# Gates summed as logarithms, with TensorE adding up the first eight chunks

## The chip, the cores and the metric

The kernel runs on one core of a Trainium2 chip. The metric is the device time in microseconds (us). A core has TensorE (PE; its weight loads are listed as PEld), VectorE (DVE), ScalarE (ACT), GpSimd (POOL) and SyncE (SP, which issues the transfers here). Each works through its own queue in order and waits for the others by semaphores.

## The reference

A gated linear recurrence per head, and then a feed-forward block with the mish function on its outputs:

```python
f = 1.0 / (1.0 + np.exp(-f_logit))             # q, k, v, f_logit: (4, 8, 768, 48)
for t in range(S):
    state = f[:, :, t, :, None] * state + np.einsum('bhd,bhe->bhde', k[:, :, t], v[:, :, t])
    y[:, :, t] = np.einsum('bhd,bhde->bhe', q[:, :, t], state)
x = y.transpose(0, 2, 1, 3).reshape(B * S, H * D)   # 3072 tokens x 384
h = x @ w_in                                        # 384 -> 2048
g = h * np.tanh(np.log1p(np.exp(h)))                # h over 20 taken as it is
out = g @ w_out                                     # 2048 -> 384
```

## The kernel before

**Chunks.** The recurrence is cut into 24 chunks of 128 tokens: six blocks of tokens for each of four batches, chunk n being block n // 4 of batch n % 4. Within a chunk the product of the gates from the chunk's start, called the decay, turns the recurrence into matmuls: k is divided by the decay, q multiplied by it, and scores, a causal mask, and the state at the chunk's start give y. A chunk's tensors lie as 128 channels (two heads of 64 places) by 4 pairs of heads by 128 tokens, so 128 x 512.

For a chunk, `attend()` adds four steps to the plan. The first loads l (the logits, from fl), k and q (L333) and v (L336), and prepares them in `prep`. There ScalarE takes exp(-l) and adds one (L351, L352), VectorE makes the running product of these with a scan (L354), which is the inverse of the decay, and ScalarE takes its logarithm and the exponential of the negative (L357, L358), the decay, into a PSUM bank. A polishing step on VectorE follows: l becomes inverse times decay (L273), and L362 corrects the decay with that and flips its sign. k times the inverse runs on GpSimd (L273; on VectorE in chunk 0), q times the decay on VectorE (L273). L365 keeps the decay at the chunk's end. Chunks 0 to 3 are loaded and prepared in two halves of 256 columns, the rest in one piece.

The other steps: transposes of k (L410) and their copy (L413); the chunk's own update of the state (L427), the scores (L385) and the mask (L391), and mid and tmp, states within and after the chunk (L441, L444, L446); the outputs (L462, L474), the new state (L490), and the output's split into a high and a low part (L500, then L503 and L505 for chunks 0 to 3, L507 for the others), which together are the tile xt. Every four chunks make one group of 512 tokens; transfers (L513) fill the last places of xt, and only then can the feed-forward part take that group.

**The feed-forward part** runs over 96 units: a group g of 512 tokens by a slice j of 128 of the 2048 hidden columns. A unit is nine matmuls 128 x 512 into h (L212), nine steps of mish (L222 to L230) on ScalarE, VectorE and GpSimd, ending in g (L228) and its high and low parts (L229, L230), and nine matmuls into o (L235). Groups 0 and 1 take turns with half of the slices each, since the weights arrive and are split into high and low parts meanwhile (`split_w`: L316 and L323 on ScalarE; L318, L319, L321, L324 on VectorE); later groups have the weights at hand.

**Order.** All work is added to a `Plan` with estimated costs and the tiles it reads and writes; `Plan.order` packs it by a simulated list schedule and gives each engine's queue its order. `attend_goal(u)` says how many attention steps are added ahead of unit u. While TensorE has nothing to do at the start, `Plan.issue` puts filler matmuls on zeros into its queue (L304, fp32 128 x 128, two instructions each) up to the first unit's L235.

PSUM has three banks `at`, two `h` and three `o`. Chunks 0 to 3 use pairs of all three kinds, later chunks only the first two `at` banks, for the decay, then scores, then outputs; the third is for transposes and updates.

## Time and profile before

| | us |
|---|---|
| median of 3 runs | 536.96 (534.45 to 538.31) |
| the profiled execution | 537.24 |
| its span, first to last instruction | 535.5 |
| busy: TensorE, VectorE, ScalarE, GpSimd | 512.4, 382.8, 415.5, 174.2 |

The profile is one execution with a record for each instruction. Busy time is the time in which an engine had an instruction running; TensorE's matmuls overlap, and its fillers count as busy too. The granted TensorE clock is given as a share of 2.4 GHz; its mean was 0.994.

### The profile page before, as it was taken

To read this page: it belongs to the slowest core of one execution; us is meant where nothing else is said; L and a number is where in the kernel's file an instruction comes from. 1 tells how busy PE (TensorE), PEld (TensorE's weight loads), DVE (VectorE), ACT (ScalarE), POOL (GpSimd) and SP (SyncE) were. 2 spreads that over 40 slices of the span, in tenths; PEclk is the share of its full clock that TensorE was granted. 3 is DMA by queue.
4 is the path that set the end of the run, shared out by engine and by line. 5 is a ranking of instruction groups with operands and counts; after the bars stand their busy time and mean duration, and the time that the engine had idled before them with its cause. 6 is when DMAs were issued, how large, how long until landed. Compare 5 with 4: busy or idle time off the path is not lost.

```text
span 535.5 us, 13156 instructions
## 1 busy us (share of the span) xinstructions
PE 512.4 (96%) x5362; PEld 408.3 (76%) x5362; DVE 382.8 (71%) x617; ACT 415.5 (78%) x746; POOL 174.2 (33%) x153
## 2 busy tenths in 40 slices
PE   7899989899998999999999999999999999999992
PEld 7787767677777777787877777787787778788881
DVE  5988999999996878785767577747565763645441
ACT  7767877799878878878887878878788776777770
POOL 2311332233234434333443333333241322132330
PEclk9999999999999999999999999999999999999997
DMA  7876444424520443231213232202221000100001
GB/s 232 283 242 234 147 138 144 151 87 156 169 74 2 140 139 110 65 115 41 61 40 109 59 102 80 60 21 89 66 94 41 2 1 31 38 21 2 1 1 66
DMA packets 23926, 48.92 MB, mean 91 GB/s; under 512 B 2800, under 2 KB 6256, under 8 KB 23856
## 3 DMA queue, kind: packets, MB, share of 16 engines
q1 hardware_dynamic: 23856, 47.98, 28.1%
q8 instruction: 44, 0.72, 0.5%
q14 instruction: 26, 0.21, 0.1%
HBM read 39.32 MB, written 6.29 MB: 85 GB/s over the span
## 4 chain that ended last, share of the span: by engine, by line
PE 68%; DVE 16%; ACT 6%; DMA 4%; issue 4%; SPq 0%; DVEq 0%; ACTq 0%
PE h L212 31%; PE o L235 29%; DVE n L224 3%; DMA l<-fl 2%; DVE g L225 2%; DVE g L228 2%; PE at L427 2%; DVE wl L324 2%; PE at L462 2%; PE at L474 2%; DVE wt L319 2%; PE at L385 1%; DVE wt L321 1%; DMA xt<-xt 1%; PE at L410 1%
## 5 line engine op out<-in xcount | busy, mean ns | idle before, releaser
L230 POOL TENSOR_TENSOR gl<-g,gh 128x512 fp32r<-128x512 f32 x96 | 128.3, 1337 | 265.9 <-ACT gh L229 247.6
L212 PE MATMUL h<-xt,wh 128*128 128x512 f32 x576 | 185.2, 402 | 8.4 <-DVE g L228 5.3
L212 PEld LDWEIGHTS h<-xt,wh 128*128 128x128 f32 x576 | 104.6, 188 | 37.0 <-DVE g L228 9.2
L235 PE MATMUL o<-gh,wh 128*128 128x512 f32 x288 | 116.0, 403 | 0.0
L212 PE MATMUL h<-xt,wl 128*128 128x512 f32 x288 | 114.1, 396 | 0.1
L235 PE MATMUL o<-gl,wh 128*128 128x512 f32 x288 | 114.1, 396 | 0.0
L235 PE MATMUL o<-gh,wl 128*128 128x512 f32 x288 | 113.3, 393 | 0.0
L224 DVE SCALAR_TENSOR_TENSOR n<-n 128x512 f32<-128x512 f32 x96 | 70.7, 737 | 57.6 <-ACT n L223 57.5
L228 DVE TENSOR_TENSOR g<-g,h 128x512 f32<-128x512 f32 x96 | 65.2, 681 | 40.1 <-ACT h L227 39.7
L222 ACT ACTIVATE n<-h,hcap 128x512 f32<-128x512 f32 x96 | 65.7, 685 | 34.1 <-PE h L212 33.5
L226 ACT ACTIVATE h<-n,two 128x512 f32<-128x512 f32 x96 | 66.0, 688 | 22.7 <-DVE g L225 22.6
L229 ACT ACTIVATE gh<-g 128x512 fp32r<-128x512 f32 x96 | 60.3, 628 | 24.4 <-DVE g L228 22.2
L225 DVE TENSOR_TENSOR g<-h,n 128x512 f32<-128x512 f32 x96 | 66.0, 687 | 7.3 <-POOL gl L230 1.1
L223 ACT ACTIVATE n<-n,hcap 128x512 f32<-128x512 f32 x96 | 69.1, 720 | 2.0
L235 PEld LDWEIGHTS o<-gl,wh 128*128 128x128 f32 x288 | 54.1, 188 | 13.7 <-POOL gl L230 0.6
L212 PEld LDWEIGHTS h<-xt,wl 128*128 128x128 f32 x288 | 54.1, 188 | 13.7 <-DVE wl L324 0.5
L235 PEld LDWEIGHTS o<-gh,wh 128*128 128x128 f32 x288 | 54.1, 188 | 12.8 <-ACT ob L578 0.3
L235 PEld LDWEIGHTS o<-gh,wl 128*128 128x128 f32 x288 | 54.1, 188 | 12.4
L227 ACT ACTIVATE h<-h 128x512 f32<-128x512 f32 x96 | 55.9, 582 | 1.6
L273 POOL TENSOR_TENSOR k<-k,inv 128x512 f32<-128x512 f32 (+1 forms) x26 | 31.7, 1222 | 68.6 <-DVE inv L354 45.4
L354 DVE TENSOR_TENSOR_SCAN inv<-gate,ones 128x516 f32<-128x516 f32 (+1 forms) x28 | 31.7, 1132 | 3.4 <-ACT gate L352 3.4
L304 PE MATMUL o<-state 128*128 128x128 f32 x200 | 28.3, 297 | 1.1 <-DVE gate L288 1.1
(97 smaller groups left out, 517.1 us busy)
## 6 DMA issues: line engine op xcount, KB each, us to landing
raw<-ww SPq DMA_DIRECT2D x16, 768.0 KB, 4.7
v<-vn SPq DMA_DIRECT2D x24, 256.0 KB, 3.9
l<-fl SPq DMA_DIRECT2D x20, 256.0 KB, 2.7
k<-kk SPq DMA_DIRECT2D x20, 256.0 KB, 2.9
q<-qq SPq DMA_DIRECT2D x20, 256.0 KB, 3.3
out<-ob SPq DMA_DIRECT2D x18, 256.0 KB, 2.1
xt<-xt SPq DMA_DIRECT2D x15, 128.0 KB, 2.5
half<-ob SPq DMA_DIRECT2D x6, 256.0 KB, 2.3
```

The lines of the kernel that those rows point to most:

```text
L212: nc.tensor.matmul(h, w[:, j, a * P : (a + 1) * P], xt[:, x, a, :], start=(n == 0), stop=(n == 3 * NK - 1))
L222: ("act", T_ACT(GT, True, 1), 0, lambda: nc.scalar.activation(u, h, AF.Relu, bias=hcap, scale=-1.0)),
L223: ("act", T_ACT(GT, False, 1), 0, lambda: nc.scalar.activation(u, u, AF.Exp, bias=hcap, scale=-1.0)),
L224: ("dve", T_DVE(GT), 1, lambda: nc.vector.scalar_tensor_tensor(n, u, 2.0, u, ALU.add, ALU.mult)),
L225: ("dve", T_DVE(GT), 0, lambda: nc.vector.tensor_tensor(g, h, n, ALU.mult)),
L226: ("act", T_ACT(GT, False, 1), 0, lambda: nc.scalar.activation(h, n, AF.Ln, bias=two)),
L227: ("act", T_ACT(GT, True), 0, lambda: nc.scalar.activation(h, h, AF.Exp, scale=-1.0)),
L228: ("dve", T_DVE(GT), 0, lambda: nc.vector.tensor_tensor(g, g, h, ALU.mult)),
L229: ("act", T_ACT(GT), 0, lambda: nc.scalar.activation(gh, g, AF.Copy)),
L230: ("pool", T_POOL(GT), 1, lambda: nc.gpsimd.tensor_tensor(gl, g, gh.bitcast(F32), ALU.subtract)),
L235: nc.tensor.matmul(o, w[:, j, m * P : (m + 1) * P], x, start=(first and i == 0), stop=(last and i == 2))
L273: add("pool" if on_pool else "dve", cost, lambda: eng.tensor_tensor(dst, x, y, ALU.mult), reads, writes, port=port)
```

## The change

- Decays are summed as logarithms. The logit is held above -40 by VectorE (`F_MIN`), ScalarE takes exp(-l) and then ln(1 + .), and the running sum of that over tokens is the negative logarithm of the decay. Two exponentials give the inverse and the decay. The scan on products, the polishing product and its correction are gone, and the sign of the decay is no longer flipped (so mid, tmp and the final check of the chunk ends change signs).
- In chunks 0 to 7 (`NS`) the logits come with tokens on the partitions, from a new array ft made on the host. TensorE makes the running sum: for each pair of heads one fp32 matmul of the logarithms (as weights) with an upper triangle of ones, into the PSUM bank of the decay. This also brings the result to channels on the partitions.
- In chunks 8 to 23 VectorE makes the running sum by a scan (multiply by `go`, which is zero at each pair's first token, and add). The inverse lies in the second PSUM bank, and k times the inverse moves from GpSimd to VectorE.
- Only chunk 0 is loaded and prepared in two halves, before it was chunks 0 to 3.
- The order of the units (`TURNS`) is the same as before, written as a table. `attend_goal` adds the attention steps of chunks 4 to 7 and of chunks 12 to 23 one unit earlier.

```diff
-        (gate,), (inv1,) = (ring(nm, 1, [P, NP, C + 1]) for nm in ("gate", "inv"))
-        (kt_s,) = ring("kt", 1, [P, NP, C])
+        (kt_s,), (go,), (cum_,), (inv_s,) = (ring(nm, 1, [P, NP, C]) for nm in ("kt", "go", "cum", "inv"))
...
-            make_upper_triangular(nc, n_[0][:, 0:P], val=-1.0, diag=True)
+            make_upper_triangular(nc, tri, val=1.0, diag=True)
...
-        nc.vector.memset(gate[:, :, 0:1], 0.0)
+        nc.vector.memset(go, 1.0)
+        nc.vector.memset(go[:, :, 0:1], 0.0)
...
-                for nm, dst, src in (("l", l_, fl), ("k", k_, kk), ("q", q_, qq)):
+                for nm, dst, src in (("l", l_, ft if n < NS else fl), ("k", k_, kk), ("q", q_, qq)):
...
-                dec, kd = b[s0 // st].rearrange("p (a c) -> p a c", a=NP), [keys[s0 // st]]
-                add("act", T_ACT(w), lambda s=s: nc.scalar.activation(gate[:, s, 1:], f[:, s], AF.Exp, scale=-1.0), kf, kg)
-                add("act", T_ACT(w), lambda s=s: nc.scalar.activation(
-                    gate[:, s, 1:], gate[:, s, 1:], AF.Copy, bias=1.0), (), kg)
-                add("dve", 2 * T_DVE(w + st) - 70, lambda s=s, st=st: nc.vector.tensor_tensor_scan(
-                    inv1[:, s].rearrange("p a c -> p (a c)"), gate[:, s].rearrange("p a c -> p (a c)"),
-                    ones.broadcast_to([P, st * (C + 1)]), 0.0, ALU.mult, ALU.max), kg, ki, port=True)
-                add("act", T_ACT(w), lambda s=s, dec=dec: nc.scalar.activation(dec[:, s], inv[:, s], AF.Ln), ki, kd)
-                add("act", T_ACT(w, True), lambda s=s, dec=dec: nc.scalar.activation(dec[:, s], dec[:, s], AF.Exp, scale=-1.0), (), kd)
-                times(False, w, f[:, s], inv[:, s], dec[:, s], ki + kd, kf, port=False)
-                times(n > 0, w, k[:, s], k[:, s], inv[:, s], ki, kk_)
-                add("dve", T_DVE(w), lambda s=s, dec=dec: nc.vector.scalar_tensor_tensor(
-                    dec[:, s], f[:, s], 2.0, dec[:, s], ALU.subtract, ALU.mult), kf, kd)
-                times(False, w, q[:, s], q[:, s], dec[:, s], kd, kq, port=False)
+                dec, kd = b[s0 // st][:, 0:w].rearrange("p (a c) -> p a c", a=st), [keys[s0 // st]]
+                add("dve", 70 + w / 1.92, lambda s=s: nc.vector.tensor_scalar(f[:, s], f[:, s], F_MIN, None, ALU.max), (), kf, port=True)
+                add("act", T_ACT(w), lambda s=s: nc.scalar.activation(f[:, s], f[:, s], AF.Exp, scale=-1.0), (), kf)
+                add("act", T_ACT(w, False, 1), lambda s=s: nc.scalar.activation(f[:, s], f[:, s], AF.Ln, bias=ones), (), kf)
+                if n < NS:
+                    add("pe", 230 * st + 100, lambda s0=s0, dec=dec: [
+                        nc.tensor.matmul(dec[:, p, :], f[:, s0 + p, :], tri, start=True, stop=True) for p in range(st)
+                    ], kf, kd)
+                    cum, kc = dec, kd
+                else:
+                    cum, kc = cum_[:, s], ["cum"]
+                    add("dve", 2 * T_DVE(w) - 70, lambda s=s, cum=cum: nc.vector.tensor_tensor_scan(
+                        cum.rearrange("p a c -> p (a c)"), go[:, s].rearrange("p a c -> p (a c)"),
+                        f[:, s].rearrange("p a c -> p (a c)"), 0.0, ALU.mult, ALU.add), kf, kc, port=True)
+                if n < NS:
+                    inv, ki = inv_s[:, s], pairs("inv", ps)
+                else:
+                    inv, ki = b[1].rearrange("p (a c) -> p a c", a=NP), [keys[1]]
+                add("act", T_ACT(w, n < NS), lambda cum=cum, inv=inv: nc.scalar.activation(inv, cum, AF.Exp), kc, ki)
+                add("act", T_ACT(w, n < NS), lambda cum=cum, dec=dec: nc.scalar.activation(dec, cum, AF.Exp, scale=-1.0), kc, kd)
+                times(0 < n < NS, w, k[:, s], k[:, s], inv, ki, kk_, port=n < NS)
+                times(False, w, q[:, s], q[:, s], dec, kd, kq, port=False)
...
-                parts = 2 if n < GC else 1
+                parts = 2 if n == 0 else 1
...
-            if u < NF + HF:
-                return per + min(per, per * (u + 4) // HF)
-            if u < 2 * NF:
-                return 2 * per + min(per, per * (u - NF - HF + 1) // (NF - HF))
-            return 3 * per + per * (u - 2 * NF + 2) // NF
+            goal = per
+            for a, b in LEAD + [(NF * g - 2, NF * (g + 1) - 2) for g in range(2, NG - 1)]:
+                goal += min(per, max(0, per * (u + 1 - a) // (b - a)))
+            return goal
```

`LEAD` is [(-4, 4), (24, 32)].

## Rows read from the trace of the kernel before

**Rows 1.** Page: span, and busy time of each engine.
```profile
span 535.5 us, 13156 instructions
PE 512.4 (96%) x5362; PEld 408.3 (76%) x5362; DVE 382.8 (71%) x617; ACT 415.5 (78%) x746; POOL 174.2 (33%) x153
```

**Rows 2.** Busy time by stretches: length, engines (instructions), granted clock, DMA share, GB/s.
```profile
10.00:20.00 10.00, 8.40 (x222) 6.89 (x221) 9.25 (x18) 6.69 (x20) 3.35 (x4) 1.00 0.90 277
50.00:60.00 10.00, 9.32 (x192) 8.22 (x192) 9.29 (x16) 9.16 (x19) 2.71 (x3) 1.00 0.43 158
80.00:90.00 10.00, 9.88 (x178) 7.64 (x176) 9.83 (x16) 7.66 (x15) 2.91 (x3) 1.00 0.27 75
120.00:140.00 20.00, 20.00 (x145) 15.64 (x144) 19.44 (x30) 18.38 (x31) 7.00 (x5) 1.00 0.48 163
260.00:300.00 40.00, 40.00 (x501) 31.75 (x499) 26.61 (x45) 33.53 (x62) 16.32 (x14) 1.00 0.21 64
```

**Rows 3.** Chain that ended last, from 445 us: start, length, instructions.
```profile
445.54 6.30 PE o L235 x27
451.84 4.20 PE h L212 x18
```

**Rows 4.** TensorE's timeline: start, length, instructions [idle before <- what ended it].
```profile
43.48 0.73 PE L212 MATMUL h<-xt,wh 128*128 128x512 f32 x2 [0.90 <-DMA xt<-xt]
...
49.09 0.61 PE L304 MATMUL o<-state 128*128 128x128 f32 x4
...
50.19 0.40 PE L462 MATMUL at<-q,state 64*64 64x64 f32 x11 [0.24 <-DVE tmp L446]
...
51.92 4.18 PE L304 MATMUL o<-state 128*128 128x128 f32 x36
56.59 0.73 PE L212 MATMUL h<-xt,wh 128*128 128x512 f32 x2 [0.49 <-DVE g L228]
...
68.34 0.73 PE L212 MATMUL h<-xt,wh 128*128 128x512 f32 x2 [2.03 <-DVE g L228]
...
96.39 0.70 PE L212 MATMUL h<-xt,wh 128*128 128x512 f32 x2 [2.02 <-DMA xt<-xt]
...
110.64 0.73 PE L212 MATMUL h<-xt,wh 128*128 128x512 f32 x2 [0.38 <-DVE g L228]
...
166.44 0.73 PE L212 MATMUL h<-xt,wh 128*128 128x512 f32 x2 [1.37 <-DVE g L228]
```

**Rows 5.** Instructions by line and shape, VectorE's decays: busy us, mean ns | idle before.
```profile
L354 DVE TENSOR_TENSOR_SCAN inv<-gate,ones 128x516 f32<-128x516 f32 x20 | 25.8, 1289 | 0.0
L362 DVE SCALAR_TENSOR_TENSOR at<-l,at 128x512 f32<-128x512 f32 x20 | 13.8, 690 | 0.3
L273 DVE TENSOR_TENSOR l<-inv,at 128x512 f32<-128x512 f32 x20 | 13.7, 684 | 9.1 <-ACT at L358 9.0
L273 DVE TENSOR_TENSOR q<-q,at 128x512 f32<-128x512 f32 x20 | 13.6, 682 | 0.4
L354 DVE TENSOR_TENSOR_SCAN inv<-gate,ones 128x258 f32<-128x258 f32 x8 | 5.9, 740 | 3.4 <-ACT gate L352 3.4
L362 DVE SCALAR_TENSOR_TENSOR at<-l,at 128x256 f32<-128x256 f32 x4 | 1.6, 419 | 0.0
L273 DVE TENSOR_TENSOR k<-k,inv 128x256 f32<-128x256 f32 x2 | 0.8, 421 | 1.3 <-DMA k<-kk 1.3
```

**Rows 6.** Line L318 by itself (shortest, median, longest ns), then its group by line.
```profile
L318 DVE TENSOR_SCALAR wt<-wt x16: 547/560/1606, 11.4 to 152.1; 128x768 int32<-128x768 int32 x16
L318 DVE TENSOR_SCALAR wt<-wt 128x768 int32<-128x768 int32 x16 | 12.5, 783 | 2.0 <-ACT wt L316 2.0
```

**Rows 7.** Instructions by line and shape, ScalarE.
```profile
L223 ACT ACTIVATE n<-n,hcap 128x512 f32<-128x512 f32 x96 | 69.1, 720 | 2.0
L351 ACT ACTIVATE gate<-l 128x512 f32<-128x512 f32 x20 | 12.5, 625 | 2.5 <-DVE inv L354 2.5
L358 ACT ACTIVATE at<-at 128x512 f32<-128x512 f32 x20 | 11.6, 578 | 0.2
```

**Rows 8.** Instructions by line and shape, GpSimd's product with k.
```profile
L273 POOL TENSOR_TENSOR k<-k,inv 128x512 f32<-128x512 f32 x20 | 26.6, 1329 | 54.7 <-DVE inv L354 43.4 <-DMA xt<-xt 9.4 <-PE o L235 1.9
```

**Rows 9.** ScalarE's timeline, from 38 us.
```profile
38.24 0.92 ACT L316 ACTIVATE wt<-raw 128x768 f32<-128x768 f32 x1 [1.66 <-DMA raw<-ww]
39.07 0.64 ACT L505 ACTIVATE xt<-at 128x256 fp32r<-128x256 f32 x2
```

More of the change, by code (lines that the diff above doesn't have):

```diff
@@ L24 @@
 NP = H // 2
+NS = 8
 GC = B
@@ L31 @@
 F_PAD = 30.0
+F_MIN = -40.0
 DEC_OK = 1.0e-13
@@ L34 @@
 W_TILE = 2 * NK * P
-HF = NF // 2
+TURNS = [(0, 0, 8), (1, 0, 8), (0, 8, 16), (1, 8, 16)]
+LEAD = [(-4, 4), (24, 32)]
 LAG = 2
@@ L174, in recurrence_moe_kernel @@
     fl: bass.AP,
+    ft: bass.AP,
     kk: bass.AP,
@@ L360, in prep @@
-                times(False, w, f[:, s], inv[:, s], dec[:, s], ki + kd, kf, port=False)
-                times(n > 0, w, k[:, s], k[:, s], inv[:, s], ki, kk_)
-                add("dve", T_DVE(w), lambda s=s, dec=dec: nc.vector.scalar_tensor_tensor(
-                    dec[:, s], f[:, s], 2.0, dec[:, s], ALU.subtract, ALU.mult), kf, kd)
-                times(False, w, q[:, s], q[:, s], dec[:, s], kd, kq, port=False)
-                add("act", 110, lambda s=s, dec=dec: nc.scalar.activation(end[:, s], dec[:, s, C - 1 : C], AF.Copy),
+                kf, kk_, kq = (pairs((x, i), ps) for x in "lkq")
@@ L366, in prep @@
+                times(False, w, q[:, s], q[:, s], dec, kd, kq, port=False)
+                add("act", 110, lambda s=s, dec=dec: nc.scalar.activation(end[:, s], dec[:, :, C - 1 : C], AF.Copy),
                     kd, pairs(("end", n), ps))
@@ L440, in attn2 @@
             if n < B:
-                add("act", T_ACT(NP * 64, True), lambda: nc.scalar.activation(mid, u[0], AF.Copy, scale=-1.0),
+                add("act", T_ACT(NP * 64, True), lambda: nc.scalar.activation(mid, u[0], AF.Copy),
                     keys[:1], ["mid"])
             else:
-                add("dve", 337, lambda: nc.vector.tensor_tensor(mid, st, u[0], ALU.subtract), keys[:1] + [ks], ["mid"])
+                add("dve", 337, lambda: nc.vector.tensor_tensor(mid, st, u[0], ALU.add), keys[:1] + [ks], ["mid"])
             if not last:
-                add("dve", 337, lambda: nc.vector.tensor_tensor(tmp, u[1], mid, ALU.subtract), keys[1:] + ["mid"], ["tmp"])
+                add("dve", 337, lambda: nc.vector.tensor_tensor(tmp, u[1], mid, ALU.add), keys[1:] + ["mid"], ["tmp"])
         def attn3(n):
@@ L532, in attend @@
                 steps[s](n)
-        units = [(g, j) for js in (range(HF), range(HF, NF)) for g in range(2) for j in js]
-        units += [(g, j) for g in range(2, NG) for j in range(NF)]
+        turns = TURNS + [(g, 0, NF) for g in range(2, NG)]
+        units = [(t, g, j) for t, (g, j0, j1) in enumerate(turns) for j in range(j0, j1)]
         def attend_goal(u):
             per = 4 * GC
-            if u < NF + HF:
-                return per + min(per, per * (u + 4) // HF)
-            if u < 2 * NF:
-                return 2 * per + min(per, per * (u - NF - HF + 1) // (NF - HF))
-            return 3 * per + per * (u - 2 * NF + 2) // NF
+            goal = per
+            for a, b in LEAD + [(NF * g - 2, NF * (g + 1) - 2) for g in range(2, NG - 1)]:
+                goal += min(per, max(0, per * (u + 1 - a) // (b - a)))
+            return goal
         while done < 4 * GC:
@@ L551, in out_unit @@
         def out_unit(u):
-            g, j = units[u]
+            t, g, j = units[u]
             half = g < 2
-            first = j == 0 or (half and j == HF)
-            last = j == NF - 1 or (half and j == HF - 1)
-            part = half and j == NF - 1
+            first, last = (j == x for x in (turns[t][1], turns[t][2] - 1))
+            part = last and half and j == NF - 1
             gs = u % 3
@@ L583, in out_unit @@
                         pairs(("ob", m)), [("half", g, m) if half else ("out", g, m)], 262)
+        split = 0
         for u in range(len(units) + LAG):
             if u < len(units):
-                g, j = units[u]
-                if g == 0:
+                t, g, j = units[u]
+                if j == split:
                     split_w(j)
+                    split += 1
                 x, hs, us, gs = g % 2, u % 2, u % 2, u % 3
@@ L608, in recurrence_moe_kernel @@
         add("dve", 119, lambda: nc.vector.tensor_scalar(
-            oks, ends.rearrange("p n a b -> p (n a b)"), -DEC_OK, None, ALU.is_le),
+            oks, ends.rearrange("p n a b -> p (n a b)"), DEC_OK, None, ALU.is_ge),
             [x for n in range(NCH) for x in pairs(("end", n))], [("st", b) for b in range(B)])
@@ L700 @@
     ("fl", (NCH, P, NP, C)),
+    ("ft", (NS, C, NP, P)),
     ("kk", (NCH, P, NP, C)),
@@ L735, in _layout @@
     ww = ww.view(np.int64)
+    fl = rows(f_logit, F_PAD)
     return {
-        "fl": rows(f_logit, F_PAD),
+        "fl": fl,
+        "ft": np.ascontiguousarray(fl[:NS].transpose(0, 3, 2, 1)),
         "kk": rows(k, 0.0),
```

5 lines of the change are left out of this document (2 added, 3 removed).

## The prediction

> **What bounds the kernel now.** Read first the head of the page. TensorE is busy for 512.4 of 535.5 us, VectorE for 382.8 [rows 1]. An average over stages with different limits hides which engine sets the pace, so the table by stretches comes next [rows 2]. From 260 to 300 us TensorE is busy for all 40.00 us and VectorE for 26.61: TensorE sets the pace, and a VectorE instruction saved there is worth nothing. The end of the chain of waits looks the same: L212 and L235 follow each other without a break, 27 matmuls in 6.30 us, 0.233 us each [rows 3]. Ahead of that, VectorE is the fuller engine: 9.25 of 10 us from 10 us on, 9.29 from 50, 9.83 from 80, 19.44 of 20 from 120 [rows 2].
>
> TensorE's "busy" of 9.32 from 50 us is not all work, since L304 only fills its idle time. So TensorE's timeline tells what is lost [rows 4]. The first matmul of the feed-forward part (L212) starts at 43.48 us. After it come fillers of 0.61 and 4.18 us, and idle gaps of 0.49, 2.03 and 2.02 us: 9.3 us up to 96.4 us. Two later gaps of 0.38 and 1.37 us are worth naming, and after 166.44 us there is none. Most gaps end at g L228, the last VectorE step on a tile of the feed-forward part; one ends at the copy xt<-xt, so at the attention of chunk 7. Both wait on work that queues on VectorE.
>
> Thus two things can be won: the 43.48 us ahead of the first L212, and about 11 us of holes behind it. All other time is TensorE's own work.
>
> **The change, part by part. VectorE, first eight chunks.** Before, a chunk of 512 columns takes the scan 1.289, the product with l 0.684, L362 0.690 and the product with q 0.682 us: 3.35 us. In two halves (chunks 0 to 3) it takes 2 x 0.740 for the scan and six passes of 256 columns at 0.419, as L362 (the products with l and q are of its size): 3.99 us. Chunk 0 adds 2 x 0.421 for k: 4.84 us [rows 5]. After, the scan, the product with l and L362 are gone, and a maximum against a constant comes in.
>
> The trace has no such maximum. Its nearest row is L318, also one tensor and a constant, 768 columns: median 0.560, longest 1.606, mean 12.5 / 16 = 0.783 us [rows 6]. From 256 to 512 columns, L362 grows by 0.271 us, which leaves 0.148 fixed; L318 at 768 columns then runs at about half that price per column. So 512 columns take about 0.42 undisturbed; with L318's mean excess of 0.22, 0.64. I take 0.55, as most L318 lie near the median. Bounds are 0.42 and 1.6.
>
> With q at 0.682 a chunk then takes 1.23 us. Chunks 4 to 7 save 2.1 each, 8.5 us; chunks 1 to 3 save 2.76 each, 8.3 us; chunk 0 has two half maxima of about 0.4, and q and k as before, 2.5 us, so it saves 2.3. Together 19.1 us, 10.6 of it ahead of the first L212 and 8.5 behind it.
>
> **TensorE.** Each of these chunks gets four fp32 matmuls with the triangle, of the shape of the filler: 4.18 us for 36 instructions, two to an fp32 matmul, so 0.232 each [rows 4], so 0.93 us a chunk. Those of chunks 0 to 3 stand where fillers stand now and cost nothing; were the fillers gone, 3.7 us. Those of chunks 4 to 7 add 3.7 us to an engine that has 9.3 us of holes there.
>
> **ScalarE.** Four long passes stay four. The plain copy (nearest row L351, 0.625) becomes a logarithm with a bias tile (nearest row L223, 0.720), and the two exponentials read PSUM or write it (L358, 0.578) [rows 7]. That is +0.1 us a chunk; in chunks 1 to 3, whose eight half passes become four whole ones, less. I take nothing; TensorE's holes cover it, at most 0.8 us without them.
>
> **Chunks 8 to 23.** VectorE loses the product with l and L362 (1.37) and gains the maximum (0.55) and the product with k (0.69, the exponential lies in PSUM as for l): 0.13 us less each. GpSimd loses 1.33 us each [rows 8]. All of it lies where TensorE is never idle, so nothing; if TensorE had holes there, 2 us at most. The second PSUM bank is now taken from the inverse decay on, but the first was taken from L357 on before, and both come free with the same evacuations (L500, L507); no new order.
>
> **Loads.** ft has as many bytes as fl. Chunks 1 to 3 come in one part, nine issues fewer on SyncE. A whole chunk must now land before its first pass, half of that was enough before. Attention's goals come one unit earlier in the list that the planner sorts: nothing to the sum, but the orders on all queues are made anew, SyncE's and GpSimd's among them.
>
> **The sum.** *Start.* The 10.6 us saved ahead of 43.48 us bound the gain above; below it is nothing, if loads set the pace: between 10 and 20 us the DMA engines are busy for 0.90 of the time, beside VectorE's 9.25 of 10 [rows 2]. With both near full I take somewhat under half: 4.5 us. One detail shows how orders matter here: the low half of the last input (L505) starts at 39.07 us, right behind L316, for whose raw weights ScalarE stood 1.66 us [rows 9]. *43 to 97 us.* Of the 9.3 us of holes, 8.5 us of VectorE relief could fill nearly all, but the chains from engine to engine stay; I let 3.7 us remain, so 5.6 are recovered, less 3.7 for the new matmuls: 1.9. *Later holes.* 1 of 1.75 us. Sum 7.4 us. The profiled execution took 537.24 us with its span of 535.5, so 529.8; the median of the runs shown, 536.96, lies 0.3 lower: **529.5 us**. With start and holes won entirely the sum is 10.6 + 9.3 - 3.7 + 1.75 = 18.0, or 519; with nothing won and 3.7 lost, 541.
>
> One behaviour speaks against this: L318, with the same work each time, takes from 0.547 to 1.606 us [rows 6]. The Trainium skill ("SBUF — State Buffer", Who interferes with whom) says that a VectorE tensor_scalar in its two-port mode and a GpSimd instruction lock each other out for a whole instruction. The spread of L318 agrees with that, though no row names the lock.
>
> **Rivals.** *A, as forecast*, 524 to 532, chance 0.53.
>
> *B, the relief is hidden.* Loads, or ScalarE (9.16 of 10 us busy from 50 us [rows 2]), set the pace ahead of 97 us; VectorE just waits. For it speaks the DMA share of 0.90; against it the gaps that end at VectorE's L228. The start wins 1, the holes take up the new matmuls: about 536. Chance 0.27.
>
> *C, slower: TensorE's queue stalls at the new matmuls.* They wait for ScalarE's logarithm, and ScalarE is nearly full; what stands behind them are L212 and L235 of the feed-forward tiles, and then every engine that works on those. If each of chunks 4 to 7 stalls TensorE by as much as its longest gap of now, 2.03 us [rows 4], that is 8.1 us; with the 3.7 of work 11.8, and the start and holes won by nothing: 549. It decides once the stalls and the work exceed what A wins, 7.4 + 3.7 = 11.1 us. Against it: today's waits for chunk work on TensorE (L427, L462) never show a gap over 0.24 us in the stretch of the chunks 4 to 7 [rows 4]. Chance 0.13. The Trainium skill ("TensorE: Matmul & The Clock Gate", Part 2) has weight loads pulled ahead but matmuls in program order, the condition for such a stall; no row here shows a matmul that overtakes another.
>
> *D, the maximum is locked out by GpSimd.* Each of the first eight at 1.6 (L318's longest) instead of 0.55 takes back 8.4 of 19.1 us of relief, so that much of the 7.4: 3.3 us, 533. For it speaks the one long L318; against it the median. Chance 0.07. The sentence on the Trainium skill's lock above belongs to this case.
>
> That the change doesn't do what it says, a longer chain for a chunk, can't be much: a pass by TensorE of 0.93 stands for a scan of 1.29, two passes of VectorE are gone.
>
> **How the numbers follow.** Likeliest is A, 529.5. About 1%, 5.4 us, is what a measurement of this kernel can tell from none. A lies nearly all under 531.6 (0.51), D and B by 0.03; slower than 542.3 are C's 0.12 and 0.01 of B: faster 0.54, same 0.33, slower 0.13. The range from 521 to 541 leaves out C nearly whole and 0.05 of wins beyond A: about 2 in 10.
>
> **What the profile after would show.** Right: the first L212 near 39 us; fillers and gaps between it and unit 8 near 4 us instead of 9.3; no scan in the first eight chunks; 64 new matmul instructions of about 0.12 us a piece; VectorE's total ahead of 100 us lower by about 19 us; the stretch behind unchanged. Wrong in the start: first L212 near 43 with VectorE idle ahead of it and DMA as the releaser. Wrong by C: gaps on TensorE ahead of the new matmuls that end at ScalarE's logarithm. Wrong by D: a maximum with a mean near 1.6 us. A new gap of TensorE after 166 us would make the whole sum wrong, since I let that stretch stand still.

## The result and the profile after

The changed kernel takes 531.59 us in the median of 15 runs (529.03 to 534.67), the kernel before 537.15 beside it (533.71 to 542.06): a ratio of 0.9907, with a 95% interval of 0.9884 to 0.993. So the change is worth 0.7 to 1.2%, about 5 us. The forecast was 529.5, the range 521 to 541. Medians and ratios, here and in the table below, leave out the few executions that took far longer than the others of their kernel (564 us and more).

The profiled execution took 533.71 us, 3.5 less than that of before. The head of its page, to be held against [rows 1]:

```profile
span 531.9 us, 13034 instructions
PE 512.8 (96%) x5358; PEld 409.7 (77%) x5358; DVE 369.7 (70%) x588; ACT 415.4 (78%) x731; POOL 157.4 (30%) x134
```

VectorE is relieved by 13 us, and the span is 3.6 us shorter. Where the rest went is seen when the time is cut at two matmuls: the first L219 (L212 before) of unit 0, at 44.39 us, and that of unit 8, the first of group 1, at 93.06. Unit 8 can't start before the attention of chunks 4 to 7 is done. Table by stretches (length; PE, PEld, DVE, ACT, POOL busy with instructions; granted clock; DMA share; GB/s), first of the kernel before, cut at 43.48 and 96.39:

```profile
0.00:43.48 43.48, 38.04 (x700) 33.54 (x700) 33.29 (x66) 32.27 (x84) 10.66 (x22) 1.00 0.78 247
43.48:96.39 52.91, 47.53 (x754) 37.31 (x755) 51.66 (x81) 42.22 (x75) 16.90 (x14) 1.00 0.50 163
```

and of the changed kernel, cut in the same places, with two stretches of 10 us (the first answers to [rows 2]):

```profile
0.00:44.39 44.39, 37.87 (x743) 33.36 (x743) 25.95 (x49) 31.09 (x69) 9.87 (x19) 0.96 0.76 250
44.39:93.06 48.67, 47.46 (x708) 38.31 (x709) 45.56 (x72) 42.94 (x77) 17.09 (x13) 1.00 0.55 180
...
10.00:20.00 10.00, 7.07 (x212) 6.00 (x208) 3.68 (x10) 6.66 (x15) 1.88 (x2) 0.95 0.79 290
20.00:30.00 10.00, 10.00 (x271) 8.37 (x273) 8.16 (x14) 8.91 (x21) 4.38 (x4) 0.88 0.62 192
```

Up to unit 8 VectorE worked 33.29 + 51.66 = 84.95 of 96.39 us before, and 25.95 + 45.56 = 71.51 of 93.06 after. It has 13.4 us less to do and stands idle for 21.55 us instead of 11.44. So 10 of 13 us of relief turned into idle time, most of it ahead of unit 0: from 10 to 20 us VectorE now works for 3.68 us, before for 9.25. In the second stretch it is still nearly full, 45.56 of 48.67.

TensorE's timeline answers to [rows 4]:

```profile
18.09 0.57 PE L440 MATMUL at<-v,kt 64*64 64x64 f32 x22 [2.57 <-issue]
...
44.39 0.73 PE L219 MATMUL h<-xt,wh 128*128 128x512 f32 x2 [0.86 <-DMA xt<-xt]
...
50.12 1.05 PE L362 MATMUL at<-tri,l 128*128 128x128 f32 x8
51.01 3.29 PE L310 MATMUL o<-state 128*128 128x128 f32 x28
54.14 0.60 PE L423 MATMUL at<-ident,k 128*128 128x128 f32 x4
54.58 0.83 PE L310 MATMUL o<-state 128*128 128x128 f32 x6
...
65.81 0.66 PE L423 MATMUL at<-ident,k 128*128 128x128 f32 x4 [0.17 <-POOL k L277]
67.15 0.69 PE L440 MATMUL at<-v,kt 64*64 64x64 f32 x32 [0.69 <-ACT kt L426]
...
93.06 0.71 PE L219 MATMUL h<-xt,wh 128*128 128x512 f32 x2 [0.18 <-DMA xt<-xt]
...
135.13 1.22 PE L219 MATMUL h<-xt,wh 128*128 128x512 f32 x2 [2.13 <-DVE g L235]
```

From unit 0 to unit 8 the holes are fillers of 3.29 and 0.83 us and gaps of 0.17, 0.69 and 0.18: 5.2 us. Before they were 10.0: to the 9.3 that the prediction added up come the 0.24 us of [rows 4] and a gap that it left out:

```profile
77.83 0.73 PE L212 MATMUL h<-xt,wh 128*128 128x512 f32 x2 [0.39 <-DVE g L228]
```

The start isn't earlier at all. It ends at a transfer into xt, as the chain of waits of this stretch shows (start, length, what):

```profile
25.35 5.97 DMA raw<-ww
...
35.88 0.67 ACT xt L517 x2
36.54 0.02 issue
36.56 0.72 SPq L525
...
37.37 0.54 SPq L320
...
38.00 0.38 SPq L339
...
38.44 5.91 DMA xt<-xt
```

The chain's first row is a load of weights. ScalarE stands for it ahead of chunk 3's mid (L453), and TensorE stands for that mid:

```profile
31.54 0.89 ACT L322 ACTIVATE wt<-raw 128x768 f32<-128x768 f32 x1 [1.53 <-DMA raw<-ww]
```

```profile
32.76 0.33 PE L474 MATMUL at<-q,mid 64*64 64x64 f32 x2 [0.80 <-ACT mid L453]
```

Chunk 3's output is complete at 36.5 us. Then SyncE issues one of its three transfers into xt, raw weights (L320, 768 KB), logits (L339, 256 KB), and then the other two, which land 5.91 us later. In [rows 4] the same wait ends at 43.48.

### The profile page after: what moved, and what is told of

It reads as the page before. It is cut to its first block, busy times and chain, and to the rows that moved or that the text cites. A ratio compares the mean times of both kernels' runs of the same rounds, so it can differ in the third digit from the quotient of the medians.

```text
span 531.9 us, 13034 instructions
## 1 busy us (share of the span) xinstructions
PE 512.8 (96%) x5358; PEld 409.7 (77%) x5358; DVE 369.7 (70%) x588; ACT 415.4 (78%) x731; POOL 157.4 (30%) x134
## 4 chain that ended last, share of the span: by engine, by line
PE 82%; DVE 7%; DMA 3%; ACT 3%; issue 2%; SPq 0%; POOL 0%; DVEq 0%; ACTq 0%
PE h L219 35%; PE o L242 34%; PE at L486 2%; PE at L474 2%; PE at L440 2%; DMA xt<-xt 2%; PE at L423 2%; PE at L398 2%; DVE wt L325 1%; DMA raw<-ww 1%; DVE g L232 1%; DVE wl L330 1%; DVE n L231 1%; PE at L362 1%; PE o L310 1%
## 5 line engine op out<-in xcount | busy, mean ns | idle before, releaser
L237 POOL TENSOR_TENSOR gl<-g,gh 128x512 fp32r<-128x512 f32 x96 | 129.9, 1356 | 302.5 <-ACT gh L236 274.3
L219 PE MATMUL h<-xt,wh 128*128 128x512 f32 x576 | 185.9, 404 | 3.4 <-DVE g L235 2.4
L219 PEld LDWEIGHTS h<-xt,wh 128*128 128x128 f32 x576 | 105.7, 189 | 31.1 <-DVE g L235 4.8
L242 PE MATMUL o<-gh,wh 128*128 128x512 f32 x288 | 116.5, 405 | 0.0
L219 PE MATMUL h<-xt,wl 128*128 128x512 f32 x288 | 114.2, 397 | 0.0
L242 PE MATMUL o<-gl,wh 128*128 128x512 f32 x288 | 113.7, 395 | 0.0
L242 PE MATMUL o<-gh,wl 128*128 128x512 f32 x288 | 113.7, 395 | 0.0
L236 ACT ACTIVATE gh<-g 128x512 fp32r<-128x512 f32 x96 | 60.1, 627 | 16.1 <-DVE g L235 14.1
L219 PEld LDWEIGHTS h<-xt,wl 128*128 128x128 f32 x288 | 54.4, 189 | 13.3
L242 PEld LDWEIGHTS o<-gh,wh 128*128 128x128 f32 x288 | 54.0, 188 | 13.5 <-ACT ob L588 0.3
L242 PEld LDWEIGHTS o<-gl,wh 128*128 128x128 f32 x288 | 54.0, 187 | 13.3
L242 PEld LDWEIGHTS o<-gh,wl 128*128 128x128 f32 x288 | 54.1, 188 | 11.8
L519 DVE TENSOR_TENSOR xt<-at,xt 128x256 fp32r<-128x256 f32 x40 | 15.9, 418 | 13.4 <-ACT xt L512 13.2
L502 POOL TENSOR_TENSOR state<-tmp,ends 128x256 f32<-128x256 f32 x20 | 16.7, 834 | 28.6 <-PE at L474 22.1
L404 DVE TENSOR_TENSOR a<-at,causal 128x256 f32<-128x256 f32 x44 | 17.7, 418 | 7.4 <-PE at L398 7.3
```

What stands on the lines that cost most here:

```text
L219: nc.tensor.matmul(h, w[:, j, a * P : (a + 1) * P], xt[:, x, a, :], start=(n == 0), stop=(n == 3 * NK - 1))
L236: ("act", T_ACT(GT), 0, lambda: nc.scalar.activation(gh, g, AF.Copy)),
L237: ("pool", T_POOL(GT), 1, lambda: nc.gpsimd.tensor_tensor(gl, g, gh.bitcast(F32), ALU.subtract)),
L242: nc.tensor.matmul(o, w[:, j, m * P : (m + 1) * P], x, start=(first and i == 0), stop=(last and i == 2))
L404: add("dve", T_DVE(NP * CH), lambda e=e: nc.vector.tensor_tensor(a_[e], sc[e], causal[:, None, :].broadcast_to([P, NP, CH]), ALU.mult), [k ...
```

## The experiments

Each kernel is the changed one but for the diff shown, and computes the whole result. All ratios are to the kernel before on the same chip, with a 95% interval; 1% is 5.4 us. Where a diff touches a step's cost or what it reads, the planner makes a new order; the kernels whose names begin with "kept" keep the changed kernel's order on every engine but for what their diff moves.

| kernel | median us | ratio | interval | first L219 | unit 8 | VectorE idle up to unit 8 |
|---|---|---|---|---|---|---|
| before | 537.15 | 1 | | 43.48 | 96.39 | 11.4 |
| after | 531.59 | 0.9907 | 0.9884 to 0.9930 | 44.39 | 93.06 | 21.6 |
| after_again | 532.43 | 0.9891 | 0.9858 to 0.9924 | 45.00 | 93.26 | 21.9 |
| scan_4_to_7 | 525.13 | 0.9767 | 0.9725 to 0.9810 | 40.88 | 85.23 | 12.4 |
| scan_0_to_3 | 536.39 | 0.9977 | 0.9948 to 1.0006 | 41.50 | 95.37 | 16.1 |
| scan_0_to_7 | 525.58 | 0.9791 | 0.9741 to 0.9841 | 43.32 | 86.28 | 8.8 |
| kept_scan | 535.60 | 0.9959 | 0.9931 to 0.9986 | 44.43 | 96.73 | 20.6 |
| kept_twice | 534.08 | 0.9951 | 0.9925 to 0.9976 | 44.34 | 95.10 | 24.1 |
| kept_raw_late | 534.87 | 0.9952 | 0.9925 to 0.9979 | 46.21 | 95.28 | 23.9 |
| log_alone | 536.59 | 0.9976 | 0.9947 to 1.0005 | 41.33 | 95.23 | 10.6 |
| log_shares | 535.02 | 0.9934 | 0.9905 to 0.9964 | 41.56 | 94.78 | 12.9 |
| kept_xt_together | 531.37 | 0.9882 | 0.9842 to 0.9921 | 41.77 | 91.78 | 20.4 |
| other_bank | 527.35 | 0.9811 | 0.9775 to 0.9847 | 40.09 | 84.79 | 14.7 |
| parts4 | 534.68 | 0.9964 | 0.9936 to 0.9992 | 39.09 | 93.92 | 20.1 |

In all fourteen the median lies 438.5 to 442.6 us above unit 8's start: what a variant is worth is decided by then, to within some 4 us. Not quite the same work lies ahead of unit 8 in all of them: nine matmuls into o (L242, some 2.2 us) more than in the changed kernel in scan_0_to_3 and parts4, nine fewer in other_bank. The first L219 tells little: parts4 has the earliest, at 39.09, and is among the slower ones.

**The changed kernel again, and scans in place of the triangle.** after_again is the changed kernel itself, on the chip of the three that follow. In those, some of the first eight chunks take VectorE's scan of the logarithms, as chunks 8 to 23 do. The diff is that of scan_4_to_7; scan_0_to_3 has `4 <= n < NS` in both places, scan_0_to_7 `n < 0`:

```diff
-                for nm, dst, src in (("l", l_, ft if n < NS else fl), ("k", k_, kk), ("q", q_, qq)):
+                for nm, dst, src in (("l", l_, ft if n < 4 else fl), ("k", k_, kk), ("q", q_, qq)):
...
-                if n < NS:
+                if n < 4:
                     add("pe", 230 * st + 100, lambda s0=s0, dec=dec: [
```

> The changed kernel once more, to tell what of its profile belongs to the kernel. Theory 1: the 2.13 us gap at 133 us with the half clock behind it (3.4 us at 1.2 GHz, some 1.7 us lost) belongs to that one execution, which at 533.71 us was above the median of 531.59; then this profile has no half clock between 100 and 160 us and its execution takes 530 to 532 us, while the first feed-forward matmul stays at 44 to 45 us. Theory 2: it belongs to the kernel's order; then the gap and the half clock are here too, and the execution takes 533 to 534 us.

> Chunks 4 to 7 make their running sum by VectorE's scan (1.42 us each, 5.7 in all) and not by TensorE's triangle (0.93 us each, of which chunks 5 to 7, 2.7 us, stand behind the first feed-forward matmul); all else as changed. Theory 1, VectorE sets the pace between 44 and 93 us and its relief is the gain: the holes on TensorE there come back by about 5.7 us less the 2.7 of work taken off, so some 3 us slower than the changed kernel, about 534.5 us. Theory 2, TensorE sets the pace there now and the triangle only costs: some 2.7 us faster, about 529 us.

> Chunks 0 to 3 make their running sum by VectorE's scan and not by the triangle, chunks 4 to 7 by the triangle. Theory 1, the start is set by loads and by the transfers into xt: the 5.8 us more on VectorE fall into its 15 us of idle time ahead of 30 us, the first feed-forward matmul stays at 44 to 45 us, and the time within 1 us of the changed kernel. Theory 2, the start is set by the chain of the four chunks through the engines: each is longer by a scan less a triangle (1.42 - 0.93 = 0.5 us), so the first feed-forward matmul comes 1 to 2 us later, and the time is 532.5 to 533.5 us.

> All chunks make their running sum by VectorE's scan; the decays stay in the logarithm, so the product with l and its correction are still gone. This parts the gain of the logarithm from that of the triangle. Theory 1, both are worth what they take off VectorE in chunks 4 to 7 (logarithm 1.37 less a maximum of 0.49 and with the shorter scan some 0.9 us a chunk, triangle 1.42): the logarithm alone is worth less than half, 534 to 535 us. Theory 2, the triangle only costs TensorE: 528 to 530 us.

after_again answers half to each of its theories. The gap at 133 us is here too, so it belongs to the order:

```profile
135.25 0.72 PE L219 MATMUL h<-xt,wh 128*128 128x512 f32 x2 [2.14 <-DVE g L235]
```

But no lower clock follows: from 130 to 140 us the mean granted clock is 1.00 here and was 0.83 of 2.4 GHz in the changed kernel's profile, where part of that stretch thus ran at 1.2 GHz.

The three others each miss both of their theories: scan_4_to_7 and scan_0_to_7 come out below them, scan_0_to_3 above. In chunks 4 to 7 the triangle is no gain. Taken out of them, the kernel is 1.2% faster than the changed one beside it, and faster than the kernel before by 2.3%; taken out of all eight, 1.0% faster than the changed one. Taken out of chunks 0 to 3 alone, it is 0.9% slower, but with scans in chunks 4 to 7 the choice for chunks 0 to 3 makes no difference that can be told (0.9767 and 0.9791). scan_4_to_7, by stretches:

```profile
0.00:40.88 40.88, 37.88 (x752) 33.38 (x753) 30.08 (x52) 33.24 (x74) 9.49 (x19) 1.00 0.84 285
40.88:85.23 44.35, 42.41 (x663) 33.14 (x662) 42.75 (x69) 38.54 (x70) 17.79 (x14) 1.00 0.52 174
```

VectorE works 72.83 us up to unit 8, about as long as with triangles, 71.51 (which has one scan in it too, chunk 8's). But it idles 12.4 us and not 21.6. So it isn't VectorE's load that differs, but when it can work. On TensorE the 24 matmuls with the triangle between unit 0 and unit 8 are gone, and the fillers there (L310) take 1.8 us instead of 4.1.

**The same order with scans, and with the triangle twice.** Is it the triangle, or the order that is planned with it?

First kept_scan (`scan` issues VectorE's instruction; chunks 4 to 7 load from fl), then kept_twice:

```diff
-                    add("pe", 230 * st + 100, lambda s0=s0, dec=dec: [
+                    add("pe", 230 * st + 100, scan if n >= 4 else lambda s0=s0, dec=dec: [
...
-                    cum, kc = dec, kd
+                    cum, kc = (cum_[:, s] if n >= 4 else dec), kd
```

```diff
-                        nc.tensor.matmul(dec[:, p, :], f[:, s0 + p, :], tri, start=True, stop=True) for p in range(st)
+                        nc.tensor.matmul(dec[:, p, :], f[:, s0 + p, :], tri, start=True, stop=True) for _ in range(1 + (n >= 4)) for p in range(st)
```

> The order of the changed kernel is kept instruction by instruction on every engine; only chunks 4 to 7 take VectorE's running sum again (4 scans of some 1.4 us) in place of the 32 triangle matmuls. Theory T (the triangle itself costs the time, as TensorE's work and as the chain token load, maximum, Ln, triangle that its queue waits for): the 4 times 0.9 us of those matmuls leave TensorE, the 2.7 us of the three that lie behind the first feed-forward matmul come back and the holes around them with them: 525 to 529 us. Theory O (the triangle costs little; the time lies in the order of loads, weights and chunk work that the planner makes with it): the order is the same, so the first feed-forward matmul stays at 44 to 45 us and the time at 530 to 532 us.

> The order is kept; chunks 4 to 7 issue each triangle matmul twice, which adds 32 matmuls, 4 times 0.9 us of TensorE. If TensorE is what sets the time there: 2.7 to 3.7 us more, 534.5 to 535.5 us. If it waits there in any case (for the maximum or the scaled copies), the second set runs in the wait: 531 to 532.5 us.

Both theories missed with kept_scan: a scan in the very place of the triangle makes the kernel 3 to 4 us slower. VectorE has 49.64 of 52.30 us to do between unit 0 and unit 8, and TensorE waits for what follows:

```profile
54.17 0.65 PE L426 MATMUL at<-ident,k 128*128 128x128 f32 x4 [0.71 <-POOL k L277]
58.25 0.73 PE L219 MATMUL h<-xt,wh 128*128 128x512 f32 x2 [1.53 <-DVE g L235]
...
68.18 0.66 PE L426 MATMUL at<-ident,k 128*128 128x128 f32 x4 [1.11 <-POOL k L277]
```

So the forecast's mechanism is right in a given order: VectorE sets the pace there, and the triangle spares it the scan. What makes scan_4_to_7 fast must lie in its order: its scans stand elsewhere, and other work moved with them. kept_twice puts unit 8 at 95.10, 1.8 to 2.0 us later, for three further sets of 0.9 us behind unit 0. The fillers can't make room for them, since they stand in TensorE's queue as instructions (34 in this stretch, as many as before the doubling), so some 0.7 of each set is paid.

**Where the scans stand.** A triangle writes into the chunk's PSUM bank, and for chunks 4 to 7 that is the bank from which the chunk before is still reading its output. In the changed kernel chunk 5's logarithm (L359) starts at 34.26 us, and its inverse (L374) 17 us later; ScalarE's timeline:

```profile
34.26 0.72 ACT L359 ACTIVATE l<-l,ones 128x512 f32<-128x512 f32 x1
...
51.69 0.59 ACT L374 ACTIVATE inv<-at 128x512 f32<-128x512 f32 x1
```

The last reader of the bank is VectorE's L519 on chunk 4's output:

```profile
48.54 0.76 DVE L519 TENSOR_TENSOR xt<-at,xt 128x256 fp32r<-128x256 f32 x2 [0.51 <-ACT xt L512]
```

It ends at 49.30; the triangle runs at 50.12, then the inverse at 51.69, k times it on GpSimd at 52.35, and the transposes at 54.14, and TensorE has fillers meanwhile. For chunks 5, 6 and 7 the inverse comes 2.1 to 2.4 us behind the release. In scan_4_to_7 the sum goes to SBUF and doesn't need the bank. VectorE's scan of chunk 5 and the release by chunk 4's output:

```profile
38.48 1.22 DVE L367 TENSOR_TENSOR_SCAN cum<-go,l 128x512 f32<-128x512 f32 x1
...
47.24 0.41 DVE L519 TENSOR_TENSOR xt<-at,xt 128x256 fp32r<-128x256 f32 x1
```

Its inverse starts at 40.85, 6.8 us ahead of the release (8.3 and 7.5 in the next two chunks). The triangle thus makes the longest part of a chunk's preparation wait for the chunk before. other_bank tests that: the triangles of chunks 4 to 7 go into the third bank of at.

```diff
+                    if n >= GC:
+                        cum, kc = at1.rearrange("p (a c) -> p a c", a=NP), [("at", 2)]
-                        nc.tensor.matmul(dec[:, p, :], f[:, s0 + p, :], tri, start=True, stop=True) for p in range(st)
+                        nc.tensor.matmul(cum[:, p, :], f[:, s0 + p, :], tri, start=True, stop=True) for p in range(st)
```

> The triangles of chunks 4 to 7 go into the third bank of at, which is free once the chunk before has taken its mid from it, and no longer into the bank that the chunk before holds until its output is split; the order is planned anew, and this one has chunk 3's transfers together. Theory B (the triangle costs because it ties the chunk's logarithms to that bank: the inverse comes behind the release of the bank in the changed kernel, 5 to 8 us ahead of it with scans): 522 to 526 us, as good as scans there or better. Theory W (what the triangle costs is its own time on TensorE, 0.9 us for each of the three chunks behind the first feed-forward matmul, and the start was the transfers' order): 527 to 529 us. Theory O (any new order is worth some 3 us either way): outside both, 530 to 534 us.

The time, 527.35, is the one of theory W; the trace shows theory B's mechanism all the same. Chunk 5's triangle on TensorE (L365 here), its inverse on ScalarE, and the release by VectorE:

```profile
42.27 1.05 PE L365 MATMUL at<-tri,l 128*128 128x128 f32 x8
```

```profile
44.47 0.59 ACT L376 ACTIVATE inv<-at 128x512 f32<-128x512 f32 x1
```

```profile
46.30 0.42 DVE L521 TENSOR_TENSOR xt<-at,xt 128x256 fp32r<-128x256 f32 x1
```

The inverse now comes 2.3 us ahead of the release, and this kernel has the same triangles as the changed one, but unit 8 at 84.79 and VectorE idle for 14.7 us. The Trainium skill ("Perfetto Trace Analysis", Matmuls) has independent matmul groups rotate through different PSUM banks, so that one is read out while the next runs. The trace agrees: unit 8 comes 8.3 us earlier, of which some 2.2 are the nine matmuls into o that lie behind it here, and the ratio is 0.8 to 1.0% lower. But with the bank the order changed too, so not all of it is the bank's.

A rival stays beside the bank: the place of the weight loads. SyncE's fourth load of weights, in the changed kernel and in scan_4_to_7:

```profile
31.01 0.36 SPq L320 DMA_DIRECT2D raw<-ww  x1
```

```profile
20.44 0.33 SPq L320 DMA_DIRECT2D raw<-ww  x1
```

In the three fastest kernels it is issued at 18.59 (scan_0_to_7), 20.44 and 23.41 us (other_bank), in the eleven others between 30.06 and 34.94. The two raw tiles take turns, so a load waits until the slice two before it has been split; an early load can thus be a consequence of the better order as well as a cause. No run moved these loads forward in a held order.

**The transfers of the start.** Two kernels change SyncE's queue alone. In kept_xt_together, L320 and L339 of 37.37 and 38.00 us go behind the last transfer into xt. In kept_raw_late, the raw load of slice 1, issued right behind that of slice 0 at 7.9 us, goes behind chunk 3's k. First the one (`xts` holds chunk 3's steps at L525), then the other:

```diff
-        for i in self.order():
+        line = self.order()
+        for xs in self.xts:
+            at_ = [line.index(i) for i in xs]
+            lo, hi = min(at_), max(at_)
+            mid = [i for i in line[lo:hi] if self.steps[i][0] == "sp" and i not in xs]
+            for i in mid:
+                line.remove(i)
+            hi = max(line.index(i) for i in xs)
+            line[hi + 1:hi + 1] = mid
+        for i in line:
```

```diff
-        for i in self.order():
+        line = self.order()
+        line.remove(self.held)
+        line.insert(line.index(self.mark) + 1, self.held)
+        for i in line:
```

> The changed kernel's order is kept but for SyncE's queue at one place: the raw weights (768 KB) and the logits (256 KB) that stand between chunk 3's three transfers into xt go behind the last of them. Theory X (the late start is this: chunk 3's output is ready at 36.5 us in the changed kernel and in the one with scans in chunks 4 to 7 alike, but the two last transfers are issued 1.6 us later and land 5.9 us after that instead of 2.1, behind a megabyte of other data): the first feed-forward matmul comes at 40.5 to 42 us instead of 44.4 to 45.0, the time falls by 2.5 to 3.5, to 528 to 529.5 us. Rival (the start is set by the weights, whose raw load is now later, or what it gives is lost behind unit 0, where TensorE has chunks 5 to 7 to do in any case): under 1 us, 531 to 532.5 us.

> The order is kept but for one transfer: the raw weights of slice 1 (768 KB) are issued by SyncE behind chunk 3's load of k, at some 14 us, instead of right behind slice 0's at 8. Theory O, in its form that two such loads back to back keep TensorE's next instructions waiting (none between 15.3 and 18.1 us): the gap at TensorE's 448th instruction falls under 1 us, the half clock behind it goes, the first feed-forward matmul comes at 41.5 to 43 us, the time is 528.5 to 530.5 us. Rival (the gap comes from something else, or the later weights lose what it gives): the first feed-forward matmul at 44 to 46 us, 531 to 533.5 us.

kept_xt_together shows theory X for the start and the rival for the time. The transfers are issued together, and the first L219 comes at 41.77, 2.6 us earlier, with no idle time ahead of it. SyncE's and TensorE's timelines, and the table by stretches:

```profile
35.05 2.02 SPq L537 DMA_DIRECT2D xt<-xt  x3
```

```profile
41.77 0.70 PE L229 MATMUL h<-xt,wh 128*128 128x512 f32 x2
```

```profile
0.00:41.77 41.77, 37.33 (x743) 32.88 (x743) 24.93 (x47) 30.34 (x69) 9.76 (x19) 1.00 0.79 263
41.77:91.78 50.01, 47.51 (x712) 38.49 (x710) 46.46 (x76) 43.29 (x77) 17.01 (x13) 1.00 0.56 176
```

Of the 2.6 us, 1.5 are not the edit's: the first of the three transfers is issued at 35.05 us and not at 36.56, although all that stands ahead of it is as in the changed kernel. Executions of one order differ that much here (37.05 in after_again). So 1.1 us are left for the place of the two loads.

And the stretch behind it grows from 48.67 to 50.01 us: VectorE has the same 71.39 us to do up to unit 8 and idles for 20.4, and TensorE meets a new gap of 1.33 us at the transposes of chunk 5, which wait for GpSimd's product with the inverse. Ahead of that inverse ScalarE now stands 1.85 us for a slice of weights, in the changed kernel 0.19 at the same place:

```profile
47.98 0.91 ACT L332 ACTIVATE wt<-raw 128x768 f32<-128x768 f32 x1 [1.85 <-DMA raw<-ww]
```

Of 2.6 us, 1.3 are left at unit 8; the time, 0.9882, can't be told from the changed kernel's.

kept_raw_late misses both of its theories (534.87 us) and moves the wait. The gap on TensorE at 18.09 is 1.49 us instead of 2.57, but little of that is the edit's: in the four other kernels that keep this order up to there it is 1.79 to 2.87. A longer one comes behind it:

```profile
17.23 0.57 PE L448 MATMUL at<-v,kt 64*64 64x64 f32 x22 [1.49 <-issue]
...
24.60 0.58 PE L523 MATMUL at<-xt,minus 128*128 128x256 f32 x1 [3.83 <-ACT xt L520]
```

since the split of that slice stands in ScalarE's queue ahead of the chunk's work and now waits for its data:

```profile
21.87 0.89 ACT L328 ACTIVATE wt<-raw 128x768 f32<-128x768 f32 x1 [3.66 <-DMA raw<-ww]
```

A transfer can't be moved alone in an order by hand: what waits for it has to move too.

**Logarithm, whole chunks and shares.** log_alone takes the scans everywhere and undoes both the whole chunks and the new shares (`attend_goal`), log_shares undoes the whole chunks only; scan_0_to_7 is the kernel with both. parts4 undoes the whole chunks in the changed kernel with its triangles.

All three have this line (and log_alone `attend_goal` as before):

```diff
-                parts = 2 if n == 0 else 1
+                parts = 2 if n < GC else 1
```

> The change without its triangle and without its parts and shares: the decays in the logarithm with VectorE's scan in every chunk, the first group's transposes in two parts and the shares by unit as in the kernel before, and the order planned anew. If the logarithm alone is the gain: 526 to 528 us, as with scans everywhere (526.4). If the parts from the second chunk and the new shares carry part of it: 529 to 534 us.

> Scans in every chunk and the new shares by unit, but the first group in two parts as in the kernel before. The kernel with neither the new shares nor the new parts gave 536.6, the one with both 526.4. If the shares carry the ten us: 526 to 529 us. If the parts do (VectorE, ScalarE and SyncE issue 3 times as many small instructions ahead of unit 0): 533 to 537 us.

> The changed kernel with its triangles and new shares, but chunks 1 to 3 loaded and prepared in two halves again, and the order planned anew. With scans in every chunk, the halves cost 8.8 us (535.2 against 526.4). Theory P (whole chunks carry the gain, since halves take more instructions on every queue ahead of the first feed-forward matmul): 536 to 541 us, unit 8 later by 4 us or more. Rival (with the triangles VectorE is relieved in those chunks, and the halves no longer matter): 530 to 533.5 us.

The logarithm alone gives nothing that can be measured, 0.9976; its 536.59 us lie above both ranges that were expected. With the new shares it is 0.9934, and the two intervals overlap. With whole chunks too, 0.9791: these are worth 1.4%, or 0.6 to 0.7% beside the triangles (parts4 against the changed kernel, between its two theories). The tables by stretches of log_shares and of scan_0_to_7 show how:

```profile
0.00:41.56 41.56, 34.64 (x725) 30.12 (x725) 31.92 (x62) 32.68 (x86) 10.40 (x23) 0.98 0.81 257
41.56:94.78 53.22, 48.52 (x685) 38.42 (x685) 49.91 (x75) 40.70 (x72) 17.02 (x13) 0.92 0.49 163
```

```profile
0.00:43.32 43.32, 40.76 (x789) 36.48 (x789) 36.82 (x61) 32.45 (x72) 12.38 (x20) 1.00 0.85 283
43.32:86.28 42.96, 42.66 (x665) 33.59 (x665) 40.65 (x66) 39.87 (x72) 15.59 (x12) 1.00 0.53 171
```

Halves start the feed-forward part 1.8 us earlier, with VectorE at 31.92 us of work by then instead of 36.82. Behind it VectorE has 49.91 to do instead of 40.65, and unit 8 is 8.5 us later. Some 3.4 of these are the clock's in this execution: the granted clock of the stretch is 0.92 instead of 1.00, and the same matmuls of the feed-forward part (L219, L242) are busy for 35.7 us there instead of 32.3. An early first L219 is no gain when VectorE brings its work along into the stretch that it bounds.

## Why the forecast was right, and where it wasn't

The total is off by 2 us, and the forecast's likeliest case, A, is the one that came. But its terms missed, in opposite directions, so that the sum fits is luck in part. Against the profiled executions (3.6 us of span):

- **The start: 4.5 us forecast, -0.9 measured.** The step that failed is "with both near full I take somewhat under half". The bound above, VectorE's relief of 10.6 us, was read as time that the start could lose. VectorE did have less to do, 25.95 instead of 33.29 us, and idled. The sign named for this came: a first L212 near 43 with VectorE idle ahead of it and a DMA as the releaser. What held the start instead is known in part: the place of a load of 768 KB and one of 256 KB in SyncE's queue (1.1 us, kept_xt_together), ScalarE's 1.53 us for weights ahead of chunk 3's mid, and TensorE's gap of 2.57 us at 18.09, whose cause is open. The deeper error is that start and stretch were added as if independent: an earlier start is given back as far as VectorE's work is only moved behind it (parts4, log_shares) or the weights come no earlier with it (kept_xt_together).
- **Holes from unit 0 to unit 8: 5.6 us forecast, 4.8 measured** (10.0 to 5.2; the forecast left 3.7 of 9.3). The mechanism is right: kept_scan shows that in this order the triangle is worth 3 to 4 us net. What is left is mostly one wait, around chunk 5's transposes, with 4.1 us of fillers.
- **The new matmuls: 3.7 us forecast, 2.5 measured**, since chunk 4's triangle runs at 36.3, ahead of unit 0. A set takes 0.81 to 0.89 us from its start to the next instruction's, forecast 0.93; twice the matmuls cost 2 us.
- **Not foreseen:** in the stretch TensorE has 1.9 us less of other work (without holes 43.5 us, of which 2.5 are triangles; before, 42.9). Some 1.0 of it is chunk 4's scores and update (L398, L440), which now lie ahead of unit 0. With that the stretch shrank by 4.2 us; the forecast had 1.9.
- **Later holes: 1 us forecast, -0.6 measured** from unit 8 to unit 95, and +1.0 in after_again, whose gaps are the same but whose clock stays at 2.4 GHz. The gaps of over 0.15 us did not shrink: 2.34 us in all before and 2.35 after, of which 2.13 at 133 us. The forecast's "after 166.44 us there is none" overlooked one of 0.29 us at 246 us; nothing came there that the sum had left out. The end behind unit 95 is 0.9 us shorter.
- **The maximum: 0.55 us forecast, 0.490 measured** in the mean of 23, median 0.420, one of 1.353 us. In the first eight chunks, where its price counts, none took over 0.43. The groups by line, of the maximum, the triangle and the scan:

```profile
L357 DVE TENSOR_SCALAR l<-l 128x512 f32<-128x512 f32 x23 | 11.3, 490 | 1.2 <-DMA l<-ft 0.8 <-DMA l<-fl 0.4
L362 PE MATMUL at<-tri,l 128*128 128x128 f32 x48 | 7.7, 304 | 0.7 <-ACT l L359 0.5
L367 DVE TENSOR_TENSOR_SCAN cum<-go,l 128x512 f32<-128x512 f32 x16 | 22.7, 1416 | 0.0
```

- **Relief of VectorE: 19.1 us forecast.** Up to unit 8 it is 13.4, but three instructions of chunk 8 (maximum, scan and product with k, 3.1 us) now lie ahead of unit 8, and filling `go` takes 0.5: without these 17.0.
- **Rivals.** B's mechanism (loads set the pace) holds for the start in part, and kept_xt_together shows it in the stretch once the start is earlier. C didn't come: TensorE waits 0.7 us in all ahead of L362. A wait there is, though, and it lies elsewhere: the planner knows of the bank and puts the triangle where it no longer stalls, so the price is fillers and VectorE's idle time. The step "a longer chain for a chunk, can't be much" counted the passes and not the bank that the first of them now needs; how much of the loss is the bank's stays open (below). D shows in one instruction of 1.353 us; the lock of the Trainium skill ("SBUF — State Buffer", Who interferes with whom) would do that. The trace agrees: that maximum starts at 215.19 us, while GpSimd's L237 runs from 214.97 to 216.26, and the three others over 0.5 us run beside an L237 too. But the mean excludes it as a cost.

So where did the expected gain go? The difference of the changed kernel to scan_4_to_7 is 1.2 to 1.4%, 6.5 to 7.5 us. By the ratios, 0.1 to 0.25% goes with chunk 3's transfers, a further 0.7% with the bank and the order that came with it (the earlier loads of weights among it), and the last 0.4% is about what three sets of triangles cost on TensorE (kept_twice: 0.4 to 0.6%). Each ratio is uncertain by some 0.4%, so only the whole and the largest part are beyond doubt. The cut between bank, loads and order stays open: every change of a step's cost or reads makes a new order, and no run held the order while the bank was changed, as the triangle's place itself must move. How far the orders differ by chance was not measured either.

## What to carry to other kernels

Relief of an engine that sets the pace pays only where the engine can be given other work; count its idle time up to the next fixed point (here unit 8) rather than the time of the first visible event, and see that the same work lies ahead of that point. When work moves to TensorE, ask which PSUM bank it needs and who holds it: a pass that cost more on VectorE but needed no bank was the better one for chunks 4 to 7, in the order that the planner made for it. For chunks 0 to 3, which have three pairs of banks, the runs don't decide. And look for small transfers that gate TensorE and stand behind bulk loads in the issuing queue: here that was 1.1 us at the first L219, and nothing that could be told in the time.

## What was not expected of the hardware

In the changed kernel TensorE stands still from 15.5 to 18.09 us without a semaphore that the profile could name (2.57 us, "issue"). It does so behind the same matmul by count, the 222nd, in the five further kernels that keep its order up to there (1.49 to 2.87 us), behind the 221st in scan_0_to_3 (3.18 us), for 0.5 us in other_bank, and not at all in scan_4_to_7. In the kernel before and in log_shares a gap of 1.3 us at this count is put down to ScalarE. In the trace a 16 KB packet of the queue for instructions starts at 15.79 and ends at 16.70, while data is moving: from 10 to 20 us the DMA engines are busy for 0.79 of the time. That TensorE's next instructions came late behind data is a possible reading. It was not shown: such a packet runs from 14.62 to 15.72 in scan_4_to_7 as well, where TensorE does not stop, and kept_raw_late's 1.49 us lie little below the 1.79 of kept_xt_together. After the gap the granted clock falls in the changed kernel: its mean from 20 to 30 us is 0.88 of 2.4 GHz, so part of that stretch ran at the lower level of 1.2. In kept_raw_late, with 3.8 us more of standing still, the mean there is 0.66; in kept_xt_together, behind 1.79 us, it is 1.00.
